# A two-layer product whose moving tiles are read in turns from their two halves

## The chip, the cores and the metric

The kernel runs on one core of a Trainium2 chip. The metric is the device time of one execution in microseconds. Before the change the median of three runs is 2235.05 us (2235.0 to 2235.06).

The engines are named as in the profile: PE is the matrix engine (TensorE) and PEld its weight loads, DVE is VectorE, ACT is ScalarE, POOL is GpSimd, SP issues most DMAs. A matmul has a stationary operand, which is loaded into the array first, and a moving operand, of which one column after another is read from SBUF; its result goes to PSUM.

## The reference

A causal convolution over seven tokens, whose taps are softmax weights of eight heads, feeds a two-layer network without biases:

```python
# x: 8 x 4096 x 192, weight: 8 x 7, w_in: 192 x 2048, w_out: 2048 x 192
w = softmax(weight)                                   # per head, over the 7 taps
out = einsum('hk,bskhg->bshg', w, x_unfolded)         # y[s] = sum_k w[k] * x[s - 6 + k]
h = out.reshape(32768, 192) @ w_in
g = where(h >= 1, h, where(h <= -1, 0, (h + 1) ** 2 / 4))
result = g @ w_out                                    # 32768 x 192, float32
```

## The kernel before

The 32768 tokens are cut into 64 superblocks of 512 tokens (`TB = 512`). The 2048 hidden units are cut into 8 groups of 256 (`NPAIR = 8`), so that there are 512 steps `q = 8 * s + j` (superblock `s`, group `j`). Everything is held with channels on the partitions and the 512 tokens of a superblock along the free dimension.

Full precision is made of float32r products: each operand is split into a high and a low part, and high times high, low times high and high times low are added up in PSUM. The array is used as two halves of 64 rows each: partitions 0 to 63 (`TOP`) and 64 to 127 (`BOT`). Each matmul works on one half, so a matmul of the one half and one of the other run at the same time; below, two such matmuls are called a pair.

- First product, `mm1`, line 411: for each step 9 pairs. The stationary operand is a 64x128 piece of `w_in`, the moving operand a 64x512 piece of the convolved x (tiles `hi0`, `lo0`, `hi1`, `lo1`, `rh`, `rhi`, `rl`, `rlo`), the result one half of the PSUM tile `h` (128 x 2 x 512, two buffers).
- The activation between: `act_clip` (DVE, line 462), `act_square` (ACT, line 468), `act_max` (DVE, line 473), then the split by `act_hi` (ACT, line 480, tile `gh`) and `act_lo` (DVE, line 486, tile `gl`). All five work element by element on 128x1024.
- Second product, `mm2`, line 451: for each step 10 pairs, stationary a piece of `w_out`, moving 64x512 of `gh` or `gl`, added over the 8 steps of a superblock into four PSUM tiles `accm0`, `accm1`, `accr0`, `accr1` (one buffer each).
- After the last step of a superblock `evac` (lines 497 and 498) copies the four tiles to SBUF on ACT, two for `accm` and two for `accr`. POOL adds them, DVE transposes the sums in 32x32 blocks, SP stores. The last superblock goes through `evac_last`, which transposes on PE.
- The convolution of later superblocks runs beside this: DMA loads, a DVE transpose, products by taps on ACT, additions on POOL (line 230).

The order of every engine's work is written out by hand in the loop over `q` (line 825 on). On PE it is `mm1(q)`, then `mm2(q - 2)`. On ACT it is `act_hi(q - 1)`, `act_square(q)`, then the copies of `evac` where a superblock has just ended, then the convolution's products. On DVE it is `act_clip(q)`, `act_lo(q - 1)`, `act_max(q)`, then transposes.

The first superblock multiplies in plain float32 (`mm1` with the unsplit weights), and the second product of the first two superblocks too (`mm2_first`, line 429, 64x128 stationary tokens and 192 moving columns). `NF32 = 16` is the number of steps in these two superblocks.

Of the kernel before, what the change touches and what calls it, by code (L numbers as in the profile page):

```python
# [18 lines left out]
P = 128  # L19
TB = 512  # L20
# [10 lines left out]
def lightconv_then_ffn(ctx: ExitStack, tc: tile.TileContext, x, weight, w_in, w_out, out):  # L31
# [24 lines left out]
    nc = tc.nc  # L56
    B, S, D = x.shape
# [7 lines left out]
    NPAIR = NF // 2  # L65
    DR = D - P
    NG = TB // SQ + 1
    TOP, BOT = slice(0, DR), slice(DR, P)
    HALVES = (TOP, BOT)
# [62 lines left out]
    NF32 = 2 * NPAIR  # L132
# [169 lines left out]
    ident = const.tile([P, P], F32, name="ident")  # L302
# [87 lines left out]
    NQ = NSB * NPAIR  # L390
    hs, g32, gs, ghs, gls, accs = {}, {}, {}, {}, {}, {}

    def mm1(q):

        s, j = divmod(q, NPAIR)

        if q == 0:
            h = hs[q] = [ps_o.tile([P, TB], F32, name=n) for n in ("accr1", "accm0")]
        else:
            h = hs[q] = ps_h.tile([P, 2, TB], F32, name="h")  # L400
            h = [h[:, e, :] for e in range(2)]

        if s == 0:
            mms = [(WI[j], us, [xop[s][u] for u in us]) for us in ("ns", "sn", "rr")]
        else:
            mms = [(W[j][:, part], u + u, [xop[s][u, x]] * 2) for u in "nsr"
                   for part, x in ((0, "hi"), (1, "hi"), (0, "lo"))]
        for n, (w, us, x) in enumerate(mms):
            for e in range(2):
                c0 = COL[us[e]][e]  # L410
                nc.tensor.matmul(h[e], w[HALVES[e], c0:c0 + P], x[e][e],  # L411
                                 start=(n == 0), stop=(n == len(mms) - 1))

    def new_accs(s):
        accs[s] = {(a, i): ps_o.tile([P, TB], F32, name=f"acc{a}{i}")
                   for a in "mr" for i in range(2)}
# [16 lines left out]
    def mm2(q):  # L433

        s, j = divmod(q, NPAIR)
        gh, gl = ghs.pop(q), gls.pop(q)
        w, wr, k = W[j + LAG], WR[j + LAG], n_in[j + LAG]
        if j == 0:
            new_accs(s)
        m0, m1, r0, r1, r = ("m", 0, gh), ("m", 1, gh), ("m", 0, gl), ("r", 0, gh), ("r", 0, gl)  # L440
        mms = [(e, m) for ms in ((m0, m1), (r0,), (r1,), (r,)) for e in range(2) for m in ms]
        if q == NQ - 1:
            mms = [(0, m) for m in (r1, m0, m1, r, r0)] + [(1, m) for m in (r1, r, m0, m1, r0)]
        first = {a: min(n for n, (e, m) in enumerate(mms) if m[0] == a) for a in "mr"}
        last = {a: max(n for n, (e, m) in enumerate(mms) if m[0] == a) for a in "mr"}
        for n, (e, (a, part, g)) in enumerate(mms):
            c0 = k + e * P
            for i in range(2):
                st = (w[HALVES[i], part, c0:c0 + P] if a == "m"
                      else wr[HALVES[i], e].rearrange("p a d -> p (a d)"))  # L450
                nc.tensor.matmul(accs[s][a, i], st, g[HALVES[i], e, :],  # L451
                                 start=(j == 0 and n == first[a]),
                                 stop=(j == NPAIR - 1 and n == last[a]))

# [35 lines left out]
    def evac(s):  # L490

        acc = accs.pop(s)
        n = slice(0, 2 * D if s * NPAIR < NF32 else TB)
        for a in "mr":
            t = [ob.tile([P, TB], F32, name="t", bufs=4) for _ in range(2)]
            y = ob.tile([P, TB], F32, name="sum")
            nc.scalar.copy(t[0][:, n], acc[a, 0][:, n])
            nc.scalar.copy(t[1][:, n], acc[a, 1][:, n])  # L498
            if s > 0:
                nc.gpsimd.tensor_add(y[:, n], t[0][:, n], t[1][:, n])  # L500
            else:
                late.append((y[:, n], t[0][:, n], t[1][:, n]))
            sums[s, a] = y
# [32 lines left out]
    def evac_last(s):  # L536


        acc = accs.pop(s)
        half, rest = slice(0, TB // 2), slice(TB // 2, TB)  # L540
        part = {}
        for a in "rm":
            u, v = [ob.tile([P, TB], F32, name="t", bufs=4) for _ in range(2)]
            for n in (half, rest):
                nc.scalar.copy(u[:, n], acc[a, 0][:, n])
                nc.vector.tensor_tensor(out=v[:, n], in0=acc[a, 1][:, n], in1=u[:, n], op=ALU.add)
            part[a] = v
        ps = [ps_h.tile([P, 2, TB], F32, name="h")[:, 0] for _ in range(2)]
        ps += [ps_o.tile([P, TB], F32, name=f"accr{i}") for i in range(2)]
        y = [ob.tile([P, TB], F32, name="sum") for _ in range(2)]  # L550
        for b in range(TB // P):
            nc.tensor.matmul(ps[b][:, P:D], part["r"][:, b * P:(b + 1) * P], ident[:, 0:DR],  # L552
                             start=True, stop=True)
        for i in range(2):
            for b in (2 * i, 2 * i + 1):
                nc.tensor.transpose(ps[b][:, 0:P], part["m"][:, b * P:(b + 1) * P], plain)
            for b, copy in ((2 * i, nc.scalar.copy), (2 * i + 1, nc.vector.tensor_copy)):
                copy(y[i][:, b % 2 * D:(b % 2 + 1) * D], ps[b][:, 0:D])
                if i == 1:
                    (nc.sync if b % 2 else nc.scalar).dma_start(  # L560
                        out=out[s * TB + b * P:s * TB + (b + 1) * P],
                        in_=y[i][:, b % 2 * D:(b % 2 + 1) * D])
            if i == 0:
                nc.sync.dma_start(
                    out=out[s * TB:s * TB + 2 * P].rearrange("(b p) d -> p b d", p=P),
                    in_=y[i][:, 0:2 * D].rearrange("p (b d) -> p b d", b=2))
# [258 lines left out]
    for q in range(NQ + DELAY):  # L825
        s, j = divmod(q, NPAIR)
        c, i = divmod(q, 2 * NPAIR)
# [11 lines left out]
        if q < NQ:  # L839
            mm1(q)  # L840
# [7 lines left out]
        else:  # L848
            if q - 1 in gs:
                act_hi(q - 1)  # L850
            if q == NPAIR + 1:
                evac(0)
# [6 lines left out]
            if done % NPAIR == NPAIR - 1 and done >= NPAIR:  # L859
                (evac if done < NQ - 1 else evac_last)(done // NPAIR)  # L860
# [10 lines left out]
            m, r = (DELAY, DELAY + 1) if s > 1 else (NPAIR - 2, NPAIR - 1)  # L871
# [7 lines left out]
        if q == NQ - 4:  # L879
            plain = ob.tile([P, TB // SQ, SQ], F32, name="osb").rearrange("p j b -> p (j b)")[:, 0:P]  # L880
# [27 lines left out]
```

## Time and profile before

| What | Value |
|---|---|
| Median of 3 runs | 2235.05 us |
| Span of the profiled execution, first to last instruction | 2233.2 us |
| Between that span and the median | 1.85 us |
| PE busy | 2227.3 us (100%) |
| PEld busy | 1850.7 us (83%) |
| DVE busy | 2093.3 us (94%) |
| ACT busy | 1693.7 us (76%) |
| POOL busy | 1173.8 us (53%) |
| Mean granted TensorE clock | 1.000 |

The page has no other time of the profiled execution than its span, so the span is what rows are compared with, and 1.85 us are added for a time. Matmuls overlap, so the busy time of PE says only that some matmul is always under way. The rate is read from the starts of matmuls, or from their number in a stretch of time. The mean time of one matmul in a group (387 ns for 512 columns) includes its way through the array and isn't the distance to the next.

### The profile page before, as it was taken

How to read it: one execution, taken by the hardware profiler on the slowest of the kernel's cores; microseconds unless marked ns; L12 is line 12 of the kernel's file. 1: busy time of each engine (PE TensorE's matmuls, PEld its weight loads, DVE VectorE, ACT ScalarE, POOL GpSimd, SP SyncE). 2: the span in 40 equal slices, each digit the busy share in tenths (PEclk: the TensorE clock that was granted, in tenths of full speed). 3: DMA queues.
4: the chain of work that ended last, by engine and by line, in shares of the span. 5: the costliest groups of instructions: out<-in, count | busy, mean ns of one | idle time of the engine just before them, and what ended most of it. 6: DMA issues, size and time to landing. Idle time of an engine off the chain costs nothing.

```text
span 2233.2 us, 48204 instructions
## 1 busy us (share of the span) xinstructions
PE 2227.3 (100%) x19646; PEld 1850.7 (83%) x19646; DVE 2093.3 (94%) x1883; ACT 1693.7 (76%) x2153; POOL 1173.8 (53%) x868
## 2 busy tenths in 40 slices
PE   9999999999999999999999999999999999999999
PEld 6988888888888888888888888888888888888887
DVE  8899999999999999999999999999999999999998
ACT  7677877778777787777877777877778777787775
POOL 1456644556545565455664456644556545565451
PEclk9999999999999999999999999999999999999999
DMA  6222222221222212222122222222221222212211
GB/s 160 49 52 48 42 47 47 52 53 39 52 49 46 54 34 52 49 49 51 40 47 48 49 51 50 41 49 46 50 54 39 52 49 46 54 34 52 49 34 25
DMA packets 442125, 110.84 MB, mean 50 GB/s; under 512 B 410288, under 2 KB 417840, under 8 KB 441904
## 3 DMA queue, kind: packets, MB, share of 16 engines
q1 hardware_dynamic: 441744, 107.66, 24.5%
q8 instruction: 155, 2.54, 0.5%
q14 instruction: 66, 0.54, 0.1%
q10 hardware_dynamic: 160, 0.10, 0.0%
HBM read 32.84 MB, written 25.17 MB: 26 GB/s over the span
## 4 chain that ended last, share of the span: by engine, by line
PE 99%; ACT 0%; DMA 0%; DVE 0%; issue 0%; DVEq 0%; ACTq 0%
PE h L411 47%; PE accm L451 30%; PE accr L451 20%; PE accr L429 1%; PE accm L429 1%; PE accr L190 0%; PE accr L411 0%; DMA osb<-in_weight_dram 0%; PE accm L181 0%; PE h L552 0%; ACT xT L168 0%; ACT xT L165 0%; ACT xT L167 0%; PE accm L411 0%; PE h L155 0%
## 5 line engine op out<-in xcount | busy, mean ns | idle before, releaser
L230 POOL TENSOR_TENSOR y<-y,p 128x512 f32<-128x512 f32 x546 | 798.2, 1462 | 733.3 <-DVE g L473 560.7
L411 PE MATMUL h<-hi,w 64*128 64x512 f32 x4032 | 764.7, 387 | 0.0
L486 DVE TENSOR_TENSOR gl<-g,gh 128x1024 fp32r<-128x1024 f32 (+1 forms) x497 | 730.4, 1470 | 29.3 <-ACT gh L480 24.2
L468 ACT ACTIVATE g<-g 128x1024 f32<-128x1024 f32 (+1 forms) x505 | 535.5, 1061 | 234.8 <-DVE g L462 228.5
L480 ACT CAST gh<-g 128x1024 fp32r<-128x1024 f32 (+1 forms) x497 | 522.8, 1052 | 226.8 <-DVE g L473 185.2
L462 DVE TENSOR_SCALAR g<-h 128x1024 f32<-128x1024 f32 (+1 forms) x505 | 609.1, 1206 | 85.5 <-PE h L411 84.4
L451 PE MATMUL accm<-gh,w 64*128 64x512 f32 x3968 | 639.6, 387 | 0.0
L473 DVE TENSOR_TENSOR g<-h,g 128x1024 f32<-128x1024 f32 (+1 forms) x505 | 613.3, 1215 | 11.8 <-ACT g L468 4.5
L411 PEld LDWEIGHTS h<-hi,w 64*128 64x128 f32 x4032 | 561.3, 185 | 75.4
L411 PE MATMUL h<-lo,w 64*128 64x512 f32 x2016 | 613.0, 387 | 0.0
L451 PEld LDWEIGHTS accm<-gh,w 64*128 64x128 f32 x3968 | 463.6, 184 | 75.6
L451 PE MATMUL accr<-gh,wr 64*128 64x512 f32 x1984 | 414.8, 387 | 0.0
L451 PE MATMUL accr<-gl,wr 64*128 64x512 f32 x1984 | 414.8, 386 | 0.0
L451 PE MATMUL accm<-gl,w 64*128 64x512 f32 x1984 | 414.7, 387 | 0.0
L411 PEld LDWEIGHTS h<-lo,w 64*128 64x128 f32 x2016 | 371.3, 184 | 38.1 <-DMA lo<-lo 0.2
L219 ACT ACTIVATE p<-xT,wk 128x512 f32<-128x512 f32 x562 | 374.9, 709 | 0.0
L451 PEld LDWEIGHTS accm<-gl,w 64*128 64x128 f32 x1984 | 276.4, 184 | 37.9
L451 PEld LDWEIGHTS accr<-gh,wr 64*128 64x128 f32 x1984 | 276.3, 184 | 37.8
L451 PEld LDWEIGHTS accr<-gl,wr 64*128 64x128 f32 x1984 | 276.2, 184 | 37.9
L411 PE MATMUL h<-rhi,w 64*128 64x512 f32 x992 | 304.1, 386 | 0.0
L411 PE MATMUL h<-rh,w 64*128 64x512 f32 x992 | 304.1, 386 | 0.0
L500 POOL TENSOR_TENSOR sum<-t 128x512 f32<-128x512 f32 (+1 forms) x124 | 157.4, 1291 | 101.8 <-ACT t L498 101.8
(143 smaller groups left out, 1945.4 us busy)
## 6 DMA issues: line engine op xcount, KB each, us to landing
out_dram<-osb SPq DMA_DIRECT2D x366, 64.0 KB, 1.9
raw<-in_x_dram SPq DMA_DIRECT2D x334, 68.0 KB, 2.4
hi<-hi SPq DMA_DIRECT2D x126, 128.0 KB, 2.3
lo<-lo SPq DMA_DIRECT2D x126, 128.0 KB, 2.3
rhi<-rh SPq DMA_DIRECT2D x62, 128.0 KB, 2.2
rlo<-rl SPq DMA_DIRECT2D x62, 128.0 KB, 2.3
words<-in_moe_w_in_dram SPq DMA_DIRECT2D x16, 192.0 KB, 3.6
words<-in_moe_w_out_dram SPq DMA_DIRECT2D x8, 384.0 KB, 4.8
```

The lines of the kernel that those rows point to most:

```text
L219: nc.scalar.mul(p, self.xT[:, SH + k:SH + k + TB], wk[:, self.wsel, k:k + 1])
L230: nc.gpsimd.tensor_add(y, y, self.product(k))
L411: nc.tensor.matmul(h[e], w[HALVES[e], c0:c0 + P], x[e][e], start=(n == 0), stop=(n == len(mms) - 1))
L429: nc.tensor.matmul(accs[s][a, i][:, c0:c0 + D], g[half, e, b * P:(b + 1) * P], w[half, e, :], start=(j == 0 and e == 0 and b % 2 == 0), st ...
L451: nc.tensor.matmul(accs[s][a, i], st, g[HALVES[i], e, :], start=(j == 0 and n == first[a]), stop=(j == NPAIR - 1 and n == last[a]))
L462: nc.vector.tensor_scalar(out=g[:, e, :], in0=hs[q][:, e, :], scalar1=-1.0, scalar2=1.0, op0=ALU.max, op1=ALU.min)
L468: nc.scalar.activation(g[:, e, :], g[:, e, :], AF.Square, bias=0.5, scale=0.5)
L473: nc.vector.tensor_tensor(out=g[:, e, :], in0=h[:, e, :], in1=g[:, e, :], op=ALU.max)
L480: nc.scalar.copy(gh[:, e, :], gs[q][:, e, :])
L486: eng.tensor_sub(gl[:, e, :], g[:, e, :], gh[:, e, :])
L500: nc.gpsimd.tensor_add(y[:, n], t[0][:, n], t[1][:, n])
```

## The change

From the third superblock on, every matmul of both products reads its 512 moving columns in another order: column 0, column 256, column 1, column 257 and so on, that is, from the two halves of the tile in turns. In bytes the read goes 1024 forward, then 1020 back, and so on. The results are written to PSUM one after the other as before. The helper `turns` makes the reading view, and `both` gives the PSUM tile the same two-dimensional shape without moving anything. `in_turns(s)` is true for superblocks 2 to 63, so 62 of 64.

`mm1` thus leaves the tokens of `h` in another order, in which the element-by-element work goes on, and `mm2` reads `gh` and `gl` in turns once more. The token at column 4a + 2b + o of an accumulator is then 256b + 128o + a. The four ACT copies of `evac` put it right: they read PSUM in order and write SBUF with steps of 128 and 256 elements between neighbours. In `evac_last` the copies stay, and the eight transposes on PE take every fourth column of their stationary operand.

The number, the kind and the order of the instructions is the same on every engine; only the access patterns of these operands differ.

```diff
+    def turns(t):
+        return t.rearrange("p (o c) -> p c o", o=2)
+
+    def both(t):
+        return t.rearrange("p (c o) -> p c o", o=2)
+
+    def in_turns(s):
+        return s * NPAIR >= NF32
...
             for e in range(2):
                 c0 = COL[us[e]][e]
-                nc.tensor.matmul(h[e], w[HALVES[e], c0:c0 + P], x[e][e],
+                to, of = (both(h[e]), turns(x[e][e])) if in_turns(s) else (h[e], x[e][e])
+                nc.tensor.matmul(to, w[HALVES[e], c0:c0 + P], of,
                                  start=(n == 0), stop=(n == len(mms) - 1))
...
-                nc.tensor.matmul(accs[s][a, i], st, g[HALVES[i], e, :],
+                nc.tensor.matmul(both(accs[s][a, i]), st, turns(g[HALVES[i], e, :]),
...
-            nc.scalar.copy(t[0][:, n], acc[a, 0][:, n])
-            nc.scalar.copy(t[1][:, n], acc[a, 1][:, n])
+            for i in range(2):
+                to, of = t[i][:, n], acc[a, i][:, n]
+                if in_turns(s):
+                    to = to.rearrange("p (b o a) -> p a b o", b=2, o=2)
+                    of = of.rearrange("p (a b o) -> p a b o", b=2, o=2)
+                nc.scalar.copy(to, of)
...
-            nc.tensor.matmul(ps[b][:, P:D], part["r"][:, b * P:(b + 1) * P], ident[:, 0:DR],
+            nc.tensor.matmul(ps[b][:, P:D], part["r"][:, b::TB // P], ident[:, 0:DR],
...
-                nc.tensor.transpose(ps[b][:, 0:P], part["m"][:, b * P:(b + 1) * P], plain)
+                nc.tensor.transpose(ps[b][:, 0:P], part["m"][:, b::TB // P], plain)
```

## The prediction

> **What bounds the kernel now.** I read the page's busy table and its chain of waits first, then PE's work in long stretches, then single starts.
>
> ```profile
> PE 2227.3 (100%) x19646; PEld 1850.7 (83%) x19646; DVE 2093.3 (94%) x1883; ACT 1693.7 (76%) x2153; POOL 1173.8 (53%) x868
> ...
> PE 99%; ACT 0%; DMA 0%; DVE 0%; issue 0%; DVEq 0%; ACTq 0%
> ```
>
> The chain that ended last is PE for 99% of the span: matmuls stand behind matmuls. So the question is what sets the distance between two of them. The table of stretches (busy us and number of instructions of each engine, granted clock, DMA share, GB/s) gives the rate:
>
> ```profile
> core 0: us, PE busy (x) PEld busy (x) DVE busy (x) ACT busy (x) POOL busy (x), PEclk, DMA share, GB/s
> 400.00:800.00 400.00, 400.00 (x3534) 331.39 (x3532) 378.46 (x326) 304.53 (x381) 216.50 (x157) 1.00 0.25 48
> 1600.00:2000.00 400.00, 400.00 (x3532) 331.41 (x3532) 377.71 (x325) 308.58 (x388) 223.49 (x157) 1.00 0.25 47
> 1000.00:1020.00 20.00, 20.00 (x180) 16.56 (x178) 19.14 (x18) 16.30 (x21) 14.79 (x10) 1.00 0.22 44
> 2200.00:2220.00 20.00, 20.00 (x180) 16.53 (x179) 18.44 (x17) 10.66 (x11) 3.02 (x4) 1.00 0.12 21
> ```
>
> 3534 matmuls in 400 us are 226.4 ns for a pair, at full clock, early as late. With POOL busy for 14.79 of 20 us or for 3.02, and twice or half the DMA, there are 180 matmuls in 20 us. The distance is therefore no matter of other engines on the same memory. Starts in the order of time (start, us, engine, line, group) give it more exactly, and its composition:
>
> ```profile
> 22.53 1.88 PE L411 MATMUL h<-hi,gh 64*128 64x512 f32 x8
> 24.25 1.02 PE L411 MATMUL h<-rh,gh 64*128 64x512 f32 x4
> 25.11 0.33 PE L429 MATMUL accm<-wf,g 64*128 64x192 f32 x2
> 46.00 0.85 PE L429 MATMUL accm<-wf,g 64*128 64x192 f32 x8
> 50.55 0.81 PE L429 MATMUL accr<-wf,g 64*128 64x192 f32 x7
> 991.24 0.84 PE L411 MATMUL h<-hi,w 64*128 64x512 f32 x4
> 993.28 1.29 PE L451 MATMUL accm<-gh,w 64*128 64x512 f32 x8
> 994.64 0.84 PE L451 MATMUL accr<-gh,wr 64*128 64x512 f32 x4
> 995.55 0.84 PE L411 MATMUL h<-hi,w 64*128 64x512 f32 x4
> ```
>
> One step, 991.24 to 995.55, is 4.31 us for 19 pairs: 226.7 ns each. The plain float32 matmuls of the start give a scale. Six pairs of 512 columns from 22.53 to 25.11 are 430 ns a pair; 28 pairs of 192 columns from 46.00 to 50.55 are 162.5. So a float32 column costs (430 - 162.5) / 320 = 0.836 ns, and a matmul about 2 ns beside its columns. Were float32r simply twice as fast by the column, 512 columns would cost 214 + 2 = 216 ns. They cost 226.7: **10.7 ns of every pair are an excess** that the plain float32 matmuls don't have.
>
> [...]
>
> Where does the excess sit? Not in the weight load, as far as rows tell:
>
> ```profile
> L411 PEld LDWEIGHTS h<-hi,w 64*128 64x128 f32 x4032 | 561.3, 185 | 75.4
> L429 PEld LDWEIGHTS accm<-wf,g 64*128 64x128 f32 x256 | 25.9, 187 | 2.6 <-issue 2.2 <-DVE warm L127 0.2 <-DVE g L749 0.2
> ```
>
> A 64x128 load takes 185 to 187 ns in both stages, and behind it the 192-column matmuls follow each other in 162.5 ns, so a load of this size allows a shorter distance than 226.7. What the 512-column float32r matmul has alone is a moving operand read at twice the float32 rate. That read is what the change alters.
>
> **The change, part by part.**
>
> *The matmuls.* 62 superblocks of 8 steps with 9 + 10 pairs are 9424 pairs. Each ns on a pair is thus 9.4 us. No row shows a moving operand with a step, so the price is bounded. Below: the whole excess goes, 9424 x 10.7 ns = 100.8 us. Above: the read falls back to one column at a time as in plain float32, 430 - 226.7 = 203.3 ns a pair, 1916 us. Between them lies nothing. I take the lower bound: the excess is tied to the double-rate read of neighbours by elimination, and with two places read in turns there is no run of neighbours left. This is the weakest step of the sum, since elimination says where the excess is and not that another order removes it.
>
> *What then ends last.* PE alone would come to 2233.2 - 100.8 = 2132.4 us of span, a step to 19 x 216 = 4.104 us. DVE is near:
>
> ```profile
> DVE g L462 <- PE h L411: 84.4, 136, 1.4
> DVE gl L486 <- ACT gh L480: 24.2, 60, 0.8
> ```
>
> (waiting engine and line, what it waited for, us in total, times, longest.) From 400 to 800 us DVE works 378.46 of 400 us, which is 4.075 us of a 4.307 us step: 99.3% of the shorter one. All that a faster PE can give back to DVE is its waits for `h`, 84.4 us in 136 places; the 24.2 us for `gh` stay. DVE therefore ends at 2233.2 - 84.4 = 2148.8, later than PE's 2132.4, and it decides. Clip still can't begin before its `mm1` ends, and at steps without a transpose some of the 136 waits will be left; I keep 3 us of the 84.4. With the 1.85 us around the span: 2148.8 + 3 + 1.85 = **2154 us**, 81 us less than 2235.05.
>
> *The copies out of PSUM.* ACT's order around them:
>
> ```profile
> 990.71 1.06 ACT L468 ACTIVATE g<-g 128x1024 f32<-128x1024 f32 x1 [0.85 <-DVE g L462]
> 991.68 0.56 ACT L497 COPY t<-accm 128x512 f32<-128x512 f32 x1
> 992.14 0.59 ACT L498 COPY t<-accm 128x512 f32<-128x512 f32 x1
> 992.62 0.60 ACT L497 COPY t<-accr 128x512 f32<-128x512 f32 x1
> 993.10 0.61 ACT L498 COPY t<-accr 128x512 f32<-128x512 f32 x1
> 993.57 1.08 ACT L480 CAST gh<-g 128x1024 fp32r<-128x1024 f32 x1
> ```
>
> The four take 1.89 us, 0.47 each. No row has an ACT write with such steps. Below, it costs nothing more; above, I let 512 spread elements cost what 1024 neighbours do, 0.97 us from 990.71 to 991.68, so 3.88 us for the four. The cover: the second `accm` copy ends at 992.73 and PE needs the tile at 993.28 (0.55 us to spare), the last `accr` copy ends at 993.71 and PE needs it at 994.64 (0.93 to spare). At the upper bound the second would end near 993.7, 0.4 us late, and the last near 995.7, against 994.64 + 0.4, 0.6 us late: 1.0 us for each of 61 superblocks, 61 us. Queued behind the copies is the cast of `gh`, 2.0 us later; `mm2` wants that `gh` one step on, after 995.55 + 2.04 = 997.6, and it would be done at 996.7. I take nothing, because a copy writes one element for each it reads and is paced by the 512 elements either way; the upper bound stays for the range.
>
> *The end.* Eight transposes read a stationary operand with step 4. They stand in the last 5 us, between 2228.00 and 2229.5 us; twice their time would be 1.5 us. I take nothing. Element-by-element work, POOL, DMAs and stores are untouched.
>
> **The rivals.**
>
> *A: turns cost a fetch for every column (slower).* Place: the moving read of all 9424 pairs. If two neighbouring columns now come with one access and columns from two places need two, the pair falls to the float32 distance of 430 ns: 2235 + 1916 = 4151 us. It decides from the first ns on a pair; at 10 ns it is 2329. For it: the float32 rows show a column at half rate as an existing mode of this read. Against: nothing in the trace shows that two columns share an access; it stays at three to one against.
>
> [...]
>
> *B: the excess isn't the read's order.* It may be a fixed cost of float32r (its operand formats, a change of weights at that rate). Then the pairs stay at 226.7 ns and the copies hide: 2235 us. For it: 226.7 is the same with every other engine quiet or loud, as a fixed cost would be. Against: the weight-load rows above.
>
> *C: as B, but spread writes cost double.* The copies then hold `accm` and `accr` back by 1.0 us a superblock, 61 us: 2296 us. With the gain of the forecast in place it would be 2154 + 61 = 2215, still faster.
>
> **How the numbers follow.** Forecast, 2154 us: 0.53 (part of the excess gone, or copies that eat some of it, are included; its own range is 2134, PE alone, to 2215). Rival B: 0.16, at 2235. Rival C, or a small price of the turns: 0.12, at 2240 to 2329. Rival A at its full price or near: 0.19. The range from 2134 to 2300 leaves out rival A and little more, so it holds about 8 in 10. A measurement of this kernel can tell a change from none from about 0.2% on, 4.5 us. Faster: 0.53. Within 0.2%: 0.16. Slower: 0.12 + 0.19 = 0.31.
>
> **What would show it.** In the profile after, a step of 19 pairs (the distance of one `mm1` start to the next) at 4.10 to 4.15 us and clearly over 180 matmuls in 20 us bears out the main step; 4.31 speaks for B; 8.2 us for A. DVE's wait for `h` should fall far below 84 us and PE should begin to wait, for `g` or `h`, if DVE is the new bound; a step of 4.104 us with no PE wait would make my DVE term wrong. The four copies should stay at 0.56 to 0.61 us and show no PE wait at `accm` or `accr`; 1.0 us and a PE wait there is C. The prediction is wrong if pairs keep their distance or lengthen.

## The result and the profile after

The changed kernel takes 2263.53 us (2263.18 to 2263.62) against 2235.06 us of the kernel before on the same chip: a ratio of 1.0127 with a 95% interval of 1.0113 to 1.0141. It is **slower by 28 us**, or 1.3%. The forecast was 2154 us, with 0.53 on faster.

The page of the changed kernel, its table of busy times and its chain of waits:

```profile
PE 2189.4 (97%) x19646; PEld 1862.2 (82%) x19646; DVE 2077.1 (92%) x1883; ACT 1785.3 (79%) x2153; POOL 1148.6 (51%) x868
...
DVE 26%; ACT 23%; PE 20%; issue 14%; POOL 12%; SPq 3%; DMA 1%; POOLq 0%; DVEq 0%; ACTq 0%
```

PE was 100% busy and 99% of the chain; now it has idle time (2189.4 of 2261.8 us busy), and the chain runs through DVE, ACT, PE and POOL. ACT has gained 91.6 us of work. The matmuls themselves did what was forecast. One undisturbed step, the starts of PE in order of time:

```profile
1007.23 0.80 PE L422 MATMUL h<-hi,w 64*128 64x512 f32 x4
...
1009.18 1.24 PE L462 MATMUL accm<-gh,w 64*128 64x512 f32 x8
...
1011.33 0.80 PE L422 MATMUL h<-hi,w 64*128 64x512 f32 x4
```

From `mm1` to `mm1` it is 4.10 us for 19 pairs, 215.8 ns a pair (216 below), where it was 4.31 us and 226.7 ns. The whole excess of 10.7 ns is gone. The step ahead of it shows what was paid. First ACT, then PE, at the end of a superblock:

```profile
1001.69 1.07 ACT L479 ACTIVATE g<-g 128x1024 f32<-128x1024 f32 x1
1002.66 1.95 ACT L513 COPY t<-accm 128x512 f32<-128x512 f32 x2
1004.42 2.01 ACT L513 COPY t<-accr 128x512 f32<-128x512 f32 x2
1006.23 1.05 ACT L491 CAST gh<-g 128x1024 fp32r<-128x1024 f32 x1
```

```profile
1003.77 0.48 PE L462 MATMUL accm<-gh,w 64*128 64x512 f32 x1
1004.66 1.13 PE L462 MATMUL accm<-gh,w 64*128 64x512 f32 x7 [0.41 <-ACT t L513]
...
1005.85 0.38 PE L462 MATMUL accr<-gh,wr 64*128 64x512 f32 x1
1006.48 0.70 PE L462 MATMUL accr<-gh,wr 64*128 64x512 f32 x3 [0.26 <-ACT t L513]
```

From the start of the first copy at 1002.66 to the start of the cast of `gh` behind them at 1006.23 are 3.57 us, where it was 1.89. PE waits twice, because `accm1` and then `accr1` haven't been read yet: the starts are 0.89 and 0.63 us apart where 0.22 would do. The waits of the whole execution (waiting engine and line, what for, us, times, longest):

```profile
DVE gl L497 <- ACT gh L491: 140.4, 106, 2.2
PE accm L462 <- ACT t L513: 48.0, 90, 0.8
...
PE accr L462 <- ACT t L513: 15.7, 61, 0.3
DVE g L473 <- PE h L422: 10.8, 34, 1.1
```

DVE waited 24.2 us for `gh` before and 140.4 now. Its wait for `h` fell from 84.4 to 10.8, as the prediction said it should. From the starts of PE, as a mean over 29 pairs of superblocks (16 steps each): 12 steps take 4.10 us, the two steps at the ends of the superblocks 5.41 and 6.37, and two more 4.69 and 4.25. Against before, 16 x 0.206 = 3.30 us are won and 4.32 lost in every pair of superblocks, so 1.02 us net, about 32 us for 31 pairs (the two spans differ by 28.6).

### The profile page after: what moved, and what is told of

It reads as the page before. It is cut to its first block, busy times and chain, and to the rows that moved or that the text cites. A ratio compares the mean times of both kernels' runs of the same rounds, so it can differ in the third digit from the quotient of the medians.

```text
span 2261.8 us, 48144 instructions
## 1 busy us (share of the span) xinstructions
PE 2189.4 (97%) x19646; PEld 1862.2 (82%) x19646; DVE 2077.1 (92%) x1883; ACT 1785.3 (79%) x2153; POOL 1148.6 (51%) x868
## 3 DMA queue, kind: packets, MB, share of 16 engines
q1 hardware_dynamic: 441744, 107.66, 24.2%
## 4 chain that ended last, share of the span: by engine, by line
DVE 26%; ACT 23%; PE 20%; issue 14%; POOL 12%; SPq 3%; DMA 1%; POOLq 0%; DVEq 0%; ACTq 0%
POOL y L230 11%; PE h L422 9%; DVE g L484 8%; ACT t L513 8%; DVE g L473 8%; DVE gl L497 7%; ACT g L479 6%; ACT gh L491 5%; PE accm L462 5%; PE accr L462 4%; DVE osb L538 2%; SPq L95 2%; ACT p L219 2%; POOL lo L252 2%; DMA raw<-in_x_dram 1%
## 5 line engine op out<-in xcount | busy, mean ns | idle before, releaser
L230 POOL TENSOR_TENSOR y<-y,p 128x512 f32<-128x512 f32 x546 | 799.8, 1465 | 757.9 <-DVE g L484 539.8
L497 DVE TENSOR_TENSOR gl<-g,gh 128x1024 fp32r<-128x1024 f32 (+1 forms) x497 | 727.5, 1464 | 151.4 <-ACT gh L491 140.4
L422 PE MATMUL h<-hi,w 64*128 64x512 f32 x4032 | 701.6, 377 | 0.0
L462 PE MATMUL accm<-gh,w 64*128 64x512 f32 x3968 | 614.0, 381 | 48.0 <-ACT t L513 48.0
L473 DVE TENSOR_SCALAR g<-h 128x1024 f32<-128x1024 f32 (+1 forms) x505 | 604.8, 1198 | 11.6 <-PE h L422 10.8
L422 PEld LDWEIGHTS h<-hi,w 64*128 64x128 f32 x4032 | 522.7, 186 | 50.5
L462 PEld LDWEIGHTS accm<-gh,w 64*128 64x128 f32 x3968 | 439.1, 186 | 128.4 <-ACT t L513 78.3
L422 PE MATMUL h<-lo,w 64*128 64x512 f32 x2016 | 541.7, 376 | 0.0
L462 PE MATMUL accr<-gh,wr 64*128 64x512 f32 x1984 | 390.4, 382 | 15.7 <-ACT t L513 15.7
L462 PE MATMUL accm<-gl,w 64*128 64x512 f32 x1984 | 380.0, 382 | 3.2
L462 PE MATMUL accr<-gl,wr 64*128 64x512 f32 x1984 | 374.1, 376 | 0.0
L422 PEld LDWEIGHTS h<-lo,w 64*128 64x128 f32 x2016 | 330.4, 186 | 25.8
L462 PEld LDWEIGHTS accm<-gl,w 64*128 64x128 f32 x1984 | 248.6, 186 | 44.3 <-DVE gl L497 23.1
```

Source lines behind the costliest of these rows:

```text
L230: nc.gpsimd.tensor_add(y, y, self.product(k))
L422: nc.tensor.matmul(to, w[HALVES[e], c0:c0 + P], of, start=(n == 0), stop=(n == len(mms) - 1))
L462: nc.tensor.matmul(both(accs[s][a, i]), st, turns(g[HALVES[i], e, :]), start=(j == 0 and n == first[a]), stop=(j == NPAIR - 1 and n == las ...
L473: nc.vector.tensor_scalar(out=g[:, e, :], in0=hs[q][:, e, :], scalar1=-1.0, scalar2=1.0, op0=ALU.max, op1=ALU.min)
L497: eng.tensor_sub(gl[:, e, :], g[:, e, :], gh[:, e, :])
```

## The experiments

The theory after this result, S: the copies that write SBUF with steps are the only thing that eats the gain, by the time that they take on ACT.

**Plain copies.** The copies of the changed kernel write in order again; what would put the tokens back is left out.

```diff
-                if in_turns(s):
-                    to = to.rearrange("p (b o a) -> p a b o", b=2, o=2)
-                    of = of.rearrange("p (a b o) -> p a b o", b=2, o=2)
                 nc.scalar.copy(to, of)
```

> The changed kernel with the four copies out of PSUM in order again, so that the tokens of superblocks 2 to 62 stay in the order of the turns in the result (putting them back is left out). Theory S (the spread copies alone eat the gain): pairs stay at 216.0 ns, the copies go back to 0.56 to 0.61 us, all PE waits at accm and accr vanish, and the time is PE's alone, 2134 to 2145 us. Rival D (DVE is the new bound, as predicted): steps of 4.14 us on average, 2150 to 2160 us. Rival P (a shorter step alone brings PE to tiles that aren't ready, whatever the copies cost): 2220 us or more.

Measured: 2170.14 us, ratio 0.9709 (0.9692 to 0.9727). S holds in the main: 93.4 us lie in the copies, and rival P is out. The time isn't PE's alone, though, so the copies aren't the only thing that eats the gain; 2170 lies above even rival D's 2150 to 2160. That rest is taken up below.

**Spread copies alone.** The kernel before, with the copies of the change and no other part of it.

```diff
-            nc.scalar.copy(t[0][:, n], acc[a, 0][:, n])
-            nc.scalar.copy(t[1][:, n], acc[a, 1][:, n])
+            for i in range(2):
+                to, of = t[i][:, n], acc[a, i][:, n]
+                if s * NPAIR >= NF32:
+                    to = to.rearrange("p (b o a) -> p a b o", b=2, o=2)
+                    of = of.rearrange("p (a b o) -> p a b o", b=2, o=2)
+                nc.scalar.copy(to, of)
```

> The kernel before with the spread copies alone: matmuls read in order, and the copies of superblocks 2 to 62 write with the steps of the change (the result's tokens are then out of place). Theory S: the copies take 1.08 to 1.11 us instead of 0.57 to 0.61, 0.90 apart instead of 0.47, PE waits for accm and accr in each of 61 superblocks, 0.8 to 1.0 us by the margins of the trace before (0.55 and 0.93 us): 2285 to 2296 us. Rival P: at the old step the copies still hide, below 2245 us.

Measured: 2308.97 us, ratio 1.0331 (1.0315 to 1.0347). That is 73.9 us, 1.21 us for each of 61 superblocks. It is rival C of the prediction as it was set up there (2296 us). S is right on the direction and the place, and low on the size. The groups and a wait of this run:

```profile
L502 ACT COPY t<-accr 128x512 f32<-128x512 f32 x122 | 125.3, 1133 | 0.0
L502 ACT COPY t<-accm 128x512 f32<-128x512 f32 x122 | 121.7, 1104 | 0.0
```

```profile
DVE gl L486 <- ACT gh L480: 131.4, 113, 2.1
```

The margins of `accm` and `accr` explain 0.8 to 1.0 us. By the starts, the steps with the copies take 5.16 and 5.86 us in turn, where 4.31 would do. The first, 0.85 us more, is what the margins said. In the second the first copy starts 1.16 us behind the start of `mm1`, where it is 0.44 in the other and 0.37 to 0.56 in the kernel before, so less of the copies is covered. A likely cause of that delay is the cast of `gh` behind the copies, for which DVE waits 131.4 us here; no run isolates it.

**Gathering on the PSUM side.** The same permutation, but the steps stand on the read.

```diff
-                    to = to.rearrange("p (b o a) -> p a b o", b=2, o=2)
-                    of = of.rearrange("p (a b o) -> p a b o", b=2, o=2)
+                    to = to.rearrange("p (v a) -> p v a", v=4)
+                    of = of.rearrange("p (a v) -> p v a", v=4)
```

> The changed kernel with the copies turned round: they read PSUM with a step of 4 columns (16 bytes) and write SBUF in order, with the same result. Theory W (what costs in the copy is the write with steps): the copies are back at 0.57 to 0.61 us and the time is that of plain copies, 2134 to 2160 us. Rival R (a step on either side costs the same): copies at 1.1 us and about 2263 us.

Measured: 2169.62 us, ratio 0.9708 (0.9693 to 0.9723). It leaves nothing out and is the **fastest complete kernel of this study, 2.9% faster than before**. Its copies:

```profile
L513 ACT COPY t<-accr 128x512 f32<-128x512 f32 x122 | 66.3, 606 | 0.0
L513 ACT COPY t<-accm 128x512 f32<-128x512 f32 x122 | 64.3, 579 | 0.0
```

They cost what plain copies cost (605 and 579 ns in the run of plain copies). Theory W holds: reading PSUM with a step of 16 bytes costs this copy nothing, writing SBUF with the steps of the change does (1113 and 1079 ns in the changed kernel).

**Copies issued twice.** Is it ACT's time, or do the spread writes disturb others?

```diff
                 nc.scalar.copy(to, of)
+                if in_turns(s):
+                    nc.scalar.copy(to, of)
```

> The changed kernel with plain copies, each of the four issued twice over (the result's tokens stay in the order of the turns; putting them back is left out). It takes ACT as long as the spread copies did, 8 x 0.47 = 3.8 us for a superblock against 4 x 0.90 = 3.6, and has no write with steps. Theory S (ACT's time for the copies, and nothing else, holds PE back): as the changed kernel, 2255 to 2280 us, PE waits at accm again. Rival M (spread writes disturb other engines' memory work): clearly nearer to plain copies at 2170, below 2225 us.

Measured: 2271.93 us, ratio 1.0164 (1.0147 to 1.0181). ACT's time alone, without any write with steps, loses as much as the change did and 8.4 us more. The run isn't an exact match, though: from the first copy to the cast of `gh` it takes 4.40 us at the median, and the spread copies 3.57. A likely reason why the longer stay costs so little more: against plain copies, DVE's subtraction (line 497) is 78.6 us shorter in all here (654.4 against 733.0), while POOL's additions are 79.1 us longer (872.4 against 793.3).

What speaks against rival M directly is that no other engine's work got more than 1% longer in the changed kernel against plain copies: DVE's max takes 1217 ns in both, clip 1200 in both, the subtraction 1467 against 1481, POOL's additions 1465 against 1453, and a pair of matmuls 216 in both. M isn't seen, and S stands.

**Write steps.** The kernel before, one step of the copies' writes for eight superblocks each.

```diff
+                step = (1, 2, 4, 8, 16, 64, 128, 256)[(s - 2) // 8] if s * NPAIR >= NF32 else 1
+                if step > 1:
+                    to = to.rearrange("p (b a) -> p a b", a=step)
+                    of = of.rearrange("p (a b) -> p a b", a=step)
                 nc.scalar.copy(to, of)
```

> The kernel before, its copies out of PSUM writing SBUF with a step of 1, 2, 4, 8, 16, 64, 128 and 256 columns between neighbours, one step for eight superblocks each (tokens stay out of place). Theory B (a write to another group of 16 bytes each time costs double): 0.57 to 0.61 us at steps 1 and 2, about 1.1 us from step 4 on. Rival C (only long steps cost): 0.6 us up to step 16, 1.1 us at 128 and 256. Rival U (every step but 1 costs double).

One execution. The `accm` copies by stretches of time, with steps of 1, 2, 4 and 128 columns in this order:

```profile
L503 ACT COPY t<-accm 128x512 f32<-128x512 f32 x16 | 8.5, 580 | 0.0
...
L503 ACT COPY t<-accm 128x512 f32<-128x512 f32 x16 | 8.9, 613 | 0.0
...
L503 ACT COPY t<-accm 128x512 f32<-128x512 f32 x16 | 15.8, 1095 | 0.0
...
L503 ACT COPY t<-accm 128x512 f32<-128x512 f32 x16 | 15.9, 1103 | 0.0
```

Theory B holds: 613 ns at 8 bytes, 1095 at 16 bytes; steps of 8, 16, 64 and 256 columns gave 1162, 1069, 1105 and 1111 ns. C and U are out.

**Read orders.** Ten orders of the moving tile, six superblocks each, with plain copies.

```diff
+    ORDERS = (("p (o c) -> p c o", dict(o=2)), ("p (o c) -> p c o", dict(o=4)),
+              ("p (c o) -> p o c", dict(o=2)), ("p (c o) -> p o c", dict(o=4)),
+              ("p (c o) -> p o c", dict(o=16)),
+              ("p (o c r) -> p c o r", dict(o=2, r=2)), ("p (o c r) -> p c o r", dict(o=2, r=4)),
+              ("p (o c r) -> p c o r", dict(o=2, r=16)), ("p (o c r) -> p c o r", dict(o=2, r=64)),
+              None)
```

> The changed kernel with plain copies and with ten read orders of the moving tile in turn, one for six superblocks each from superblock 2 on (the result's tokens stay in these orders, putting them back is left out): columns from 2 places in turns, from 4 places in turns, every 2nd column, every 4th, every 16th, runs of 2, 4, 16 and 64 columns from 2 places in turns, and in order. Theory N (the excess belongs to columns that follow their neighbour): 216 ns a pair for 2 and 4 places, every 2nd, 4th and 16th; runs of 2 near 221, of 4 near 224, of 16 and 64 at 226 to 227, in order 226.7. Rival L (the excess belongs to the change from one group of some bytes to the next in one run, once in 16 columns): runs of 16 in turns are like in order, shorter runs like turns, and every 2nd column like in order or dearer. Rival F (only a single unbroken run of 512 is dear): all but the last at 216. Rival A (a fetch for each group): every 16th column and 4 places cost more than 226.7, up to 430.

One execution, 3018.8 us. Stretches inside the second to the last order, in the sequence of the list (columns as in the prediction's table; PE is busy for the whole of each):

```profile
300.00:500.00 200.00, 200.00 (x1415) 189.18 (x1413) 147.10 (x131) 124.13 (x155) 80.66 (x63) 1.00 0.19 38
600.00:900.00 300.00, 300.00 (x1332) 270.88 (x1331) 135.89 (x122) 117.05 (x146) 75.80 (x60) 1.00 0.12 24
1000.00:1300.00 300.00, 300.00 (x1303) 265.79 (x1301) 133.66 (x120) 114.52 (x143) 72.81 (x60) 1.00 0.12 24
1450.00:1700.00 250.00, 250.00 (x1157) 234.05 (x1155) 118.73 (x107) 99.49 (x123) 60.19 (x50) 1.00 0.13 24
1850.00:2050.00 200.00, 200.00 (x1203) 193.65 (x1201) 123.79 (x112) 105.51 (x132) 64.64 (x52) 1.00 0.17 32
2100.00:2290.00 190.00, 190.00 (x1523) 176.82 (x1522) 165.43 (x141) 139.75 (x170) 90.90 (x70) 1.00 0.22 43
2330.00:2500.00 170.00, 170.00 (x1420) 158.56 (x1418) 149.38 (x130) 126.01 (x160) 89.37 (x67) 1.00 0.23 45
2560.00:2700.00 140.00, 140.00 (x1238) 128.05 (x1237) 132.62 (x114) 106.91 (x135) 77.24 (x57) 1.00 0.24 47
2760.00:2960.00 200.00, 200.00 (x1768) 182.95 (x1766) 189.71 (x163) 152.53 (x191) 109.75 (x76) 1.00 0.22 44
```

Twice the length over the count is a pair: 283 ns from four places in turns; 450, 461 and 432 for every 2nd, 4th and 16th column; 333, 250 and 239 for runs of 2, 4 and 16 columns from two places; 226 for runs of 64 and in order. Single columns from two places, the first of the list, take 216 by starts in the same run. None of the four theories fits: N holds for that one, runs of 64 and in order, and fails on the others. Rival A's forecast came for the two orders that it names (283 and 432 ns), but a fetch for each group doesn't explain 216 from two places, where the group changes at each column. Single columns from **two** places are the one order here that is better than in order; nearly every other is worse. Rival A's price, the float32 distance of 430 ns, does occur, at 432 to 461 ns; the change happens not to call on it.

**Distances.** Two places in turns, at 128, 64, 32, 16, 8, 4 and 2 columns, then eight places, then in order, seven superblocks each.

```diff
+    ORDERS = tuple(("p (k o c) -> p k c o", dict(o=2, c=d)) for d in (128, 64, 32, 16, 8, 4, 2))
+    ORDERS += (("p (o c) -> p c o", dict(o=8)), None)
```

> The changed kernel with plain copies, and columns read from two places in turns at another distance for every seven superblocks: 128, 64, 32, 16, 8, 4 and 2 columns, then eight places in turns (64 columns apart), then in order (the result's tokens stay so). Theory H (what counts is that two places are far enough apart to lie in different parts of the memory, as 256 columns do): 216 ns a pair for 256 and some shorter distances down to a border, then 283 to 460; which, the run shows. Rival G (two places in turns are always good, because each group of 4 columns that was fetched is used by 4 of every 8 reads): 216 at all distances of 4 columns and more. Eight places: 283 or more by either.

One execution, 2467.95 us. Distances of 128, 4 and 2 columns, eight places, in order:

```profile
110.00:310.00 200.00, 199.34 (x1834) 182.13 (x1832) 194.25 (x169) 157.36 (x198) 108.67 (x81) 1.00 0.26 49
...
1270.00:1470.00 200.00, 199.01 (x1826) 176.68 (x1824) 194.21 (x169) 156.98 (x199) 108.52 (x82) 1.00 0.26 49
1510.00:1710.00 200.00, 200.00 (x1769) 183.16 (x1766) 189.03 (x163) 152.85 (x193) 106.42 (x78) 1.00 0.24 47
1760.00:2200.00 440.00, 440.00 (x1811) 369.61 (x1809) 184.07 (x166) 160.38 (x197) 100.47 (x81) 1.00 0.12 22
2260.00:2450.00 190.00, 190.00 (x1680) 174.07 (x1678) 177.31 (x154) 137.88 (x169) 89.39 (x64) 1.00 0.19 37
```

By starts inside `mm1` it is 216 ns a pair at every distance from 128 down to 4 columns (16 bytes) and 226.7 at 2 columns; eight places take 486 by the stretch. Rival G's forecast came and H is out: from 4 columns on, the distance is no matter. At 2 columns the four columns of two turns lie within 16 bytes, and nothing is won. G's reason, what was fetched being used again, isn't shown by this.

**The rest above PE's own time.** Two theories for 2170 against 2134: T, ACT is full in the slot ahead of the copies of every second superblock; V, DVE is short of time, since its subtraction (line 497) is long beside POOL. Where the rest lies, in the kernel that gathers on the PSUM side:

```profile
992.35 2.12 DVE L497 TENSOR_TENSOR gl<-g,gh 128x1024 fp32r<-128x1024 f32 x1
...
994.40 1.21 DVE L484 TENSOR_TENSOR g<-h,g 128x1024 f32<-128x1024 f32 x1
...
995.54 1.21 DVE L473 TENSOR_SCALAR g<-h 128x1024 f32<-128x1024 f32 x1
...
996.78 1.06 ACT L479 ACTIVATE g<-g 128x1024 f32<-128x1024 f32 x1
...
997.74 1.05 ACT L513 COPY t<-accm 128x512 f32<-128x512 f32 x2
...
998.36 0.97 PE L462 MATMUL accm<-gh,w 64*128 64x512 f32 x3 [0.33 <-ACT t L513]
```

A subtraction of 2.12 us, then DVE's max and clip without a pause, ACT's square, the copies, and PE waits for them. This step takes 4.95 us on average, once in 16.

Four runs on top of that kernel. The first moves taps of the convolution, which ACT multiplies, to later slots:

```diff
-    PLAN_R = {7: ("T",), 8: (0, 1, 2), 10: (3, 4), 11: (5, 6), 13: "split"}
+    PLAN_R = {7: ("T",), 8: (0,), 10: (1, 2), 11: (3, 4), 12: (5, 6), 14: "split"}
```

> The kernel of turns with copies that read PSUM with a step (2170 us), and with the taps of the third convolution unit moved: in slot 8 of 16 one product on ACT instead of three, the others in slots 10, 11 and 12 and its split in 14 instead of 13. Theory T (what is left, 849 + 140 us in thousandths of a us at two of 16 steps, comes from ACT being full in the slot ahead of the copies of every second superblock): most of 0.99 us of each 16 steps goes, 31 x 0.99 = 31 us at the best, so 2140 to 2155 us. Rival V (DVE, whose work fills its step, is behind there): within 6 us of 2170.

Measured: 2191.18 us, ratio 0.9802 (0.9787 to 0.9817); 21.6 us slower than without. Inconclusive by itself, since the later split makes a new wait:

```profile
PE h L422 <- DMA rlo<-rl: 16.5, 29, 1.4
```

By the starts, the step with the copies fell only from 4.95 to 4.84 us. The same with the split left in its place:

```diff
-    PLAN_R = {7: ("T",), 8: (0, 1, 2), 10: (3, 4), 11: (5, 6), 13: "split"}
+    PLAN_R = {7: ("T",), 8: (0,), 10: (1, 2, 3), 11: (4, 5, 6), 13: "split"}
```

> The same kernel with all additions, and with two of the three products of slot 8 moved to slots 10 and 11, whose products grow to three each; the split stays in slot 13, so that the high and low parts arrive in time. Theory T: ACT is free 1.4 us earlier ahead of the copies, most of the 0.85 us at that step goes, 2145 to 2155 us. Theory V: the copies wait for DVE's clip and ACT's square in front of them, so little changes: 2160 to 2175 us, in line with the 0.11 us that this step gained in the run with later taps.

Measured: 2171.58 us, ratio 0.9716 (0.9702 to 0.9731). Nothing is won. T falls here.

The third puts the copies ahead of the square on ACT:

```diff
                 act_clip(q)
-                act_square(q)
             if done % NPAIR == NPAIR - 1 and done >= NPAIR:
                 (evac if done < NQ - 1 else evac_last)(done // NPAIR)
+            if q < NQ:
+                act_square(q)
```

> The same kernel with the four copies ahead of that step's square on ACT, so that they don't wait for DVE's clip. The copies come up to 1.0 us earlier, the square 1.9 us later and with it DVE's max. If DVE has room (rival T), PE's waits at accm and accr go and the time falls to 2140 to 2155 us; if DVE is the engine that is short of time (theory V), the late square costs it about 1 us a superblock and the time rises to 2180 to 2230 us.

Measured: 2190.03 us, ratio 0.9799 (0.9784 to 0.9813), 20.4 us slower than with the square first. PE waits at `accm` and `accr` no more, and DVE's max pays:

```profile
DVE g L484 <- ACT g L479: 107.7, 72, 2.1
...
PE h L422 <- DVE g L484: 22.4, 30, 0.8
```

The fourth leaves out POOL's additions of the taps:

```diff
-                    nc.gpsimd.tensor_add(y, y, self.product(k))
+                    self.product(k)
```

> The kernel of turns with copies that read PSUM with a step (2170 us), and with the additions of the convolution's tap products on POOL left out from the second pair of superblocks on (the products on ACT stay; the result lacks these taps). Theory V (what is left above PE's 2134 us is DVE, whose subtraction takes 1.22 us alone and up to 2.3 us beside POOL): the subtraction falls from 1.48 us on average to 1.25, DVE's load by some 110 us, and the time comes to PE's 2134 to 2140 us. Rival T (ACT is full ahead of the copies of every second superblock): 2160 to 2170 us, since ACT's work is the same.

Measured: 2134.32 us, ratio 0.9549 (0.9533 to 0.9565). DVE's subtraction with POOL's additions (the kernel that gathers on the PSUM side):

```profile
L497 DVE TENSOR_TENSOR gl<-g,gh 128x1024 fp32r<-128x1024 f32 x495 | 733.1, 1481 | 50.7 <-ACT gh L491 39.5
```

and without:

```profile
L497 DVE TENSOR_TENSOR gl<-g,gh 128x1024 fp32r<-128x1024 f32 x495 | 632.3, 1277 | 39.2 <-ACT gh L491 34.1
...
DVE g L473 <- PE h L422: 63.1, 152, 1.4
```

The subtraction is 101 us shorter in all, DVE waits for PE again (63.1 us), and the time is PE's own 2134 us to a us. DVE's max, of whose inputs one lies in PSUM, stays at 1217 and 1221 ns, and ACT's work is the same (1684.5 and 1687.8 us). V is shown: what is left above PE is DVE beside POOL, 1481 against 1277 ns a subtraction. Why the subtraction takes longer beside POOL, no run shows.

## Why the prediction was right and wrong

- **The excess and its seat: right.** 10.7 ns of each pair, seen by laying the float32r matmul beside the float32 ones of two widths, belongs to the moving read, and the turns remove it (216 ns forecast, 215.8 measured). That elimination pointed to the read was right. The reason why turns should help, that "there is no run of neighbours left", was not: four and eight places in turns and every 2nd, 4th or 16th column leave none either, and take 283 to 486 ns. That this order was the one that helps was luck; it could as well have gone the other way by a factor of two.
- **PE's own time: right.** 2132.4 us of span plus 1.85 were 2134; the run without POOL's taps takes 2134.32.
- **DVE as the next bound: right in kind, low in size.** 2154 was the sum; with copies that cost nothing extra (the gather on the PSUM side) it is 2170. The step kept 3 us of DVE's 84.4 us of waits for `h` and let the 24.2 us for `gh` stay. In that run they are

```profile
DVE gl L497 <- ACT gh L491: 39.9, 102, 0.6
...
DVE g L473 <- PE h L422: 10.7, 33, 1.2
```

  so the two terms were low by 15.7 and 7.7 us, against which DVE's work came out 9.1 us shorter (2084.2 for 2093.3). PE loses time at single steps, as the rows above show: where the subtraction takes over 2 us beside POOL, clip comes late, and with it the square and the copies behind it. A mean load of 99.3% hid that.
- **The copies out of PSUM: this step failed, and it turned the sign.** "I take nothing, because a copy writes one element for each it reads and is paced by the 512 elements either way." A copy whose writes go 16 bytes or more apart takes almost twice the time: 1076 and 1111 ns at the median against 567 to 611. That costs 93.4 us, more than the 65 us that are won without it. The upper bound of the prediction, 0.97 us a copy, was near the measured 0.89 from start to start (3.57 us for four); the choice between the ends was wrong.
- **The price of that bound was low, too.** It said 1.0 us a superblock and 61 us in all, and with the gain 2215. Measured is (2263.5 - 2170.1) / 61 = 1.53 us at the faster step and 1.21 at the old one. The margins were read where the first copy starts 0.44 us behind the start of `mm1`. In the changed kernel it starts 0.83 and 1.81 us behind, in turn, and with the gather on the PSUM side as well; without POOL's additions it is 0.53 and 0.67. So most of what the cover lost, it lost to DVE beside POOL, at the faster step that fills DVE to 99.3%. Left out, too, was DVE's wait for the cast of `gh`, which was followed only as far as `mm2`, not to the subtraction that also needs it (24.2 us before, 140.4 after); its share isn't isolated. Together, 32 us of copies and 16 us of DVE are the 48 us between 2215 and 2263.5.
- **The rivals.** C had the mechanism that decided, but was set up without the gain; with the gain the text called it "still faster". Both the gain and the loss came, and the loss was the larger: 65 us won with plain copies, 93.4 lost to spread ones. The measured 2263.5 us lies in the range that the text gave to rival C or a small price of the turns, with a chance of 0.12.
- **The end: nothing was taken, 1.5 us was the bound.** The transposes with step 4 run from 2255.65 to 2258.2 us, 2.6 us where it was 1.5: 1 us, with nothing in the sum for it.

## What to carry to other kernels

When a permutation has to be undone somewhere, price it on both sides of the instruction that does it, and put the steps on the side that is free: here the same four copies cost nothing extra with the steps on the PSUM read (606 and 579 ns against 605 and 579 in order), and more than the whole gain with the steps on the SBUF write (93.4 us against 65). An unknown cost on an instruction that releases a PSUM tile is to be taken at its upper bound until a row says otherwise, and followed to everything that stands behind it in its queue, not only to the tile it frees. Compare a matmul's distance with that of another type or width in the same trace: what it takes beyond the rate that the other suggests can be found in that trace alone. It says where time is lost, not which change wins it back.

## What the runs showed of the hardware

- A float32r moving operand of 512 columns takes 226.7 ns a pair in order, and 216 if single columns come from two places in turns that are 4 to 256 columns apart. Four places take 283 ns, eight 486; every 2nd, 4th or 16th column 432 to 461. Runs from two places in turns: 333 at 2 columns, 250 at 4, 239 at 16, 226 at 64. Why two places are the best isn't shown; the only clue is that nothing is won at 2 columns' distance, where both lie within 16 bytes (226.7 ns).
- An ACT copy of 128x512 float32 from PSUM (`accm`) to SBUF takes 580 ns in order, 613 with a write step of 8 bytes and 1069 to 1162 from 16 bytes on. With a read step of 16 bytes on the PSUM side it takes 579.
- DVE's subtraction of two SBUF tiles (128x1024 float32) takes 1481 ns on average beside POOL's additions and 1277 without them, with up to 2.15 us for a single one against 1.79. With the copies issued twice, the subtraction is 78.6 us shorter in all than with plain copies and POOL's additions are 79.1 us longer: what DVE wins there, POOL loses.
